# Two chunks of a fused attention and feed-forward kernel on unsplit float32 weights, gates and activations

## Chip, core and metric

The kernel runs on one core of a Trainium2 chip. The metric is the device time of one execution in microseconds. Three executions of the kernel before took 1021.11, 1022.39 and 1024.19 us; the median is 1022.39. A fourth execution was profiled.

## What is computed

Sliding-window attention over 8 batches, 8 heads, 576 positions and 64 dimensions (each position sees itself and the 63 before it), then a feed-forward block with a rational gate on the 4608 tokens. Weights arrive as float64 and q, k, v as float32.

```python
def _attn_ref(q, k, v):
    scores = scale * np.matmul(q, k.transpose(0, 1, 3, 2))
    rel = pos[:, None] - pos[None, :]
    mask = (rel >= 0) & (rel < window)
    scores = np.where(mask, scores, -1000000000.0)
    ...
    attn = attn / (np.sum(attn, axis=-1, keepdims=True) + 1e-09)
    return np.matmul(attn, v)

def _moe_ref(x, w_in, w_out, a, b):
    h = x @ w_in                      # 4608x512 @ 512x2048
    P = a[0] + a[1] * h + a[2] * h2 + a[3] * h3
    Q = 1.0 + np.abs(b[0]) * np.abs(h) + np.abs(b[1]) * h2
    g = P / (Q + 1e-6)
    return g @ w_out                  # 4608x2048 @ 2048x512
```

## The kernel before

**Tiling.** The tokens are cut into 12 chunks of 384. The 2048 columns of the feed-forward block are cut into 16 blocks of 128. A *step* is one block of one chunk: `ffn1` multiplies the chunk's attention output x (four tiles of 128x384) by the block of w_in, the gate follows on ScalarE, VectorE and GpSimd, and three steps later (`LAG`) `ffn2` multiplies the gate's output by the block of w_out and adds it into three PSUM accumulators of 128x512. There are 192 steps. The first two chunks are taken in halves, so that they can begin while the weights still arrive: eight steps of chunk 0, sixteen of chunk 1, eight more of chunk 0, whose first half waits in `part` (L285); from step 32 on a chunk is 16 steps. At a chunk's end ScalarE copies the accumulators to `ob` (L294), and a DMA takes them out.

**Attention** is worked in *units*: two heads of one chunk, four units per chunk. `unit_scores` makes the scores on TensorE (L182), masks them and takes the maximum on VectorE (L188 to L198), six exp on ScalarE (L201), and divides (L203 to L205). `unit_transpose` transposes on TensorE (L212) and copies on ScalarE (L214). `unit_av` multiplies by v (L223). The scores and the transposes share one PSUM buffer, so one unit follows the other. All of these matmuls take plain float32 tiles.

**Precision.** The products of the feed-forward block use float32r tiles, a float32 with a shortened mantissa, in which a value is a pair: hi (the cast) and lo (what the cast left out). A product is three matmuls, lo·hi, hi·hi and hi·lo: L239 twelve times per step, L280 nine times. So each weight, each x and each gate output is cast on ScalarE and subtracted on VectorE: `decode` builds a float32 out of the float64's two words (one pass of ScalarE, L113, four of VectorE, L114 to L118) and splits it at once (L121, L122); `unit_av` does the same for x (L228, L229); the gate makes gh directly (L257) and gl as the rest of the division (L258 to L260).

**Order.** The program is written step by step. `todo` says at which step a weight is loaded or an attention unit begins; the weights of the first half come with steps 0 to 7, those of the second half one load per step from step 7 to step 22. Then a scheduler sets the order in which the instructions stand on each engine; every engine works through its own row in that order. Buffers come from pools: a tile waits until the one whose buffer it takes has been read.

Of the kernel before, what the change touches and what calls it, by code (L numbers as in the profile page):

```python
# [9 lines left out]
F32 = mybir.dt.float32  # L10
# [7 lines left out]
CH = 384  # L18
TC = CH // WIN
PR = TC // 2  # L20
DEC = 28
AHEAD = 3
# [9 lines left out]
def swa_rational_ffn(ctx: ExitStack, tc: tile.TileContext, qT, kT, v, w_in, w_out, a, b, out):  # L32
# [61 lines left out]
    wi_h = const.tile([P, NCC, DFF], F32R, name="wi_h")  # L94
    wi_l = const.tile([P, NCC, DFF], F32R, name="wi_l")
    wo_h = const.tile([P, NF, DO], F32R, name="wo_h")
    wo_l = const.tile([P, NF, DO], F32R, name="wo_l")
# [3 lines left out]
    def decode(src, hi, lo):  # L101

        w = stage.tile([P, 512, 2], U32, name="w_st", bufs=2)
        if len(src.shape) == 3:
            nc.sync.dma_start(out=w.rearrange("p (c n) two -> p c (n two)", c=src.shape[1]), in_=src)
        else:
            nc.sync.dma_start(out=w.rearrange("p n two -> p (n two)"), in_=src)
        low, high = w[:, :, 0], w[:, :, 1]
        c = stage.tile([P, 512], U32, name="w_c")
        cf = c.bitcast(F32)  # L110


        nc.scalar.activation(cf, w.bitcast(F32)[:, :, 1], AF.Abs)  # L113
        nc.vector.tensor_scalar(out=cf, in0=cf, scalar1=2.0 ** -15, scalar2=None, op0=ALU.max)  # L114

        nc.vector.tensor_scalar(out=c, in0=c, scalar1=3, scalar2=0x3FFFFFF8, op0=ALU.logical_shift_left, op1=ALU.bitwise_and)
        nc.vector.scalar_tensor_tensor(out=c, in0=low, scalar=29, in1=c, op0=ALU.logical_shift_right, op1=ALU.bitwise_or)  # L117
        nc.vector.scalar_tensor_tensor(out=c, in0=high, scalar=0xC0000000, in1=c, op0=ALU.bitwise_and, op1=ALU.bitwise_or)  # L118
        if len(hi.shape) == 3:
            cf = cf.rearrange("p (c n) -> p c n", c=hi.shape[1])  # L120
        nc.scalar.copy(out=hi, in_=cf)  # L121
        nc.vector.tensor_tensor(out=lo, in0=cf, in1=hi.bitcast(F32), op=ALU.subtract)  # L122

    def load_w_in(i):
        sl = slice(i * P, (i + 1) * P)
        decode(w_in_v[:, :, 2 * i * P:2 * (i + 1) * P], wi_h[:, :, sl], wi_l[:, :, sl])

    def load_w_out(i):
        decode(w_out_v[:, i, :], wo_h[:, i, :], wo_l[:, i, :])
# [87 lines left out]
    def unit_av(c, hp):  # L217
        u = live.pop((c, hp))

        ps = ps_a.tile([P, TC, WIN], F32, name="ps_x", bufs=1)  # L220
        for j in range(TC):
            for z in range(2):
                nc.tensor.matmul(ps[z * 64:z * 64 + 64, j, :], u["vt"][:, u["vw"][j], z * 64:z * 64 + 64],  # L223
                                 u["pT"][:, z, j * WIN:(j + 1) * WIN], start=True, stop=True)
        xh[c, hp] = xp.tile([P, CH], F32R, name=f"xh{hp}")
        xl[c, hp] = xp.tile([P, CH], F32R, name=f"xl{hp}")
        x = ps.rearrange("p t s -> p (t s)")
        nc.scalar.copy(out=xh[c, hp], in_=x)  # L228
        nc.vector.tensor_tensor(out=xl[c, hp], in0=x, in1=xh[c, hp].bitcast(F32), op=ALU.subtract)  # L229
# [4 lines left out]
    def ffn1(c, i):  # L234
        h = ps_h.tile([P, CH], F32, name="h")
        n = 0
        for cc in range(NCC):
            for w, x in ((wi_h, xl), (wi_h, xh), (wi_l, xh)):
                nc.tensor.matmul(h, w[:, cc, i * P:(i + 1) * P], x[c, cc], start=n == 0, stop=n == 3 * NCC - 1)  # L239
                n += 1  # L240
# [3 lines left out]
        gh = gp.tile([P, CH], F32R, name="gh")  # L244
        gl = gp.tile([P, CH], F32R, name="gl")
# [8 lines left out]

        nc.scalar.activation(ah, u, AF.Ln, bias=QADD)
        nc.scalar.activation(ah, ah, AF.Exp, scale=-1.0)  # L256
        nc.vector.scalar_tensor_tensor(out=gh, in0=num, scalar=a_sb[:, 0:1], in1=ah, op0=ALU.add, op1=ALU.mult)  # L257
# [12 lines left out]
    def ffn2(s):  # L270
# [6 lines left out]
        for t in range(NTS):  # L277
            ts = slice(t * P, (t + 1) * P)
            for n, (g, w) in enumerate(((gl, wo_h), (gh, wo_l), (gh, wo_h))):
                nc.tensor.matmul(acc[c][t], g[:, ts], w[:, i, :], start=first and n == 0, stop=last and n == 2)  # L280
# [3 lines left out]
        if c == 0 and c not in part:  # L284
            part[c] = const.tile([P, NTS, DO], F32, name="part")  # L285
            for t in range(NTS):
                nc.scalar.copy(out=part[c][:, t, :], in_=o[t])
            return
        for t in range(NTS):
            ob = part[0][:, t, :] if s == total - 1 else op.tile([P, DO], F32, name="ob")  # L290
            if c in part:
                nc.vector.tensor_tensor(out=ob, in0=o[t], in1=part[c][:, t, :], op=ALU.add)
# [15 lines left out]
    wi, wo = list(range(H, NF)), list(range(H, NF))  # L308
    queue = [(load_w_in, wi.pop(0)) for _ in range(WLEAD)]
    while wi or wo:  # L310
        if wi:
            queue.append((load_w_in, wi.pop(0)))
        queue.append((load_w_out, wo.pop(0)))
    for n, call in enumerate(queue):
        at(H + n - 1, *call)

# [72 lines left out]
```

## Time and profile before

| | us |
|---|---|
| median of three runs | 1022.39 |
| profiled execution, whole time | 1025.14 |
| its span, first to last instruction | 1023.3 |
| TensorE busy | 953.1 (93%) |
| TensorE weight loads busy | 840.4 (82%) |
| VectorE busy | 850.3 (83%) |
| ScalarE busy | 725.8 (71%) |
| GpSimd busy | 233.7 (23%) |
| mean granted TensorE clock | 0.978 |

Shares of the whole span hide that the run has stages: a stage has to be read by itself, by the engine that is full in it. The busy time of an instruction runs from its start to its end, and neighbours on one engine can overlap; the pace of an engine is read from start to start.

### The profile page before, as it was taken

Reading aid. Unit: us, or ns where it says so; the run is one execution under the profiler, and the core shown is the slowest. Engines: PE = TensorE matmul, PEld = TensorE weight load, DVE = VectorE, ACT = ScalarE, POOL = GpSimd, SP = SyncE. Lnnn points to the kernel's source line nnn. Section 1 sums busy time; section 2 is a strip of 40 time slices with the busy share of each in tenths; the row PEclk is TensorE's granted clock in tenths of the full one; section 3 lists DMA queues with packets and bytes.
Section 4 is the critical chain, followed back from the end, with each engine's and each line's share of the span. In section 5 each row is a group of like instructions: output and inputs, shape, how many; then the busy total and the mean of one; then the engine's idle time right before and its main releaser. Section 6 shows DMA issues by size and latency. Waiting matters only on the chain.

```text
span 1023.3 us, 18244 instructions
## 1 busy us (share of the span) xinstructions
PE 953.1 (93%) x6624; PEld 840.4 (82%) x6624; DVE 850.3 (83%) x1639; ACT 725.8 (71%) x1734; POOL 233.7 (23%) x231
## 2 busy tenths in 40 slices
PE   2677876899999999999999999999999999999997
PEld 2565755788898898898898898898898898888996
DVE  5999999998878878878878878878888888888785
ACT  4675765577767867867867867867867867866664
POOL 2000010002322322322322322322322322322221
PEclk9878989899999999999999999999999999999999
DMA  6634433111112112111112112111112112100000
GB/s 197 205 99 133 133 94 111 50 50 55 60 30 60 61 31 65 64 31 58 60 30 61 61 31 65 64 32 58 60 31 60 62 31 65 65 16 2 31 1 31
DMA packets 68537, 64.09 MB, mean 63 GB/s; under 512 B 4448, under 2 KB 61792, under 8 KB 68448
## 3 DMA queue, kind: packets, MB, share of 16 engines
q1 hardware_dynamic: 68448, 62.93, 19.8%
q8 instruction: 52, 0.85, 0.4%
q14 instruction: 37, 0.30, 0.1%
HBM read 53.48 MB, written 9.44 MB: 61 GB/s over the span
## 4 chain that ended last, share of the span: by engine, by line
PE 81%; DVE 11%; ACT 3%; DMA 3%; issue 1%; POOL 0%; SPq 0%; POOLq 0%; ACTq 0%; DVEq 0%
PE o L280 37%; PE h L239 35%; PE ps_x L223 3%; PE ps_s L182 3%; PE ps_s L212 3%; DMA w_st<-w_in 1%; DVE w_c L117 1%; DMA w_st<-w_out 1%; ACT sm L201 1%; DVE w_c L118 1%; DVE num L259 1%; DVE gh L257 1%; DVE u L258 1%; DVE num L249 1%; DVE num L250 1%
## 5 line engine op out<-in xcount | busy, mean ns | idle before, releaser
L239 PE MATMUL h<-xl,wi_h 128*128 128x384 f32 x768 | 264.9, 345 | 14.8 <-DVE num L250 8.6
L239 PE MATMUL h<-xh,wi_h 128*128 128x384 f32 x768 | 260.6, 339 | 0.0
L239 PE MATMUL h<-xh,wi_l 128*128 128x384 f32 x768 | 259.7, 338 | 0.0
L280 PE MATMUL o<-wo_h,gl 128*128 128x512 f32 x576 | 238.1, 413 | 22.3 <-DVE gl L260 22.3
L252 POOL TENSOR_TENSOR u<-u,ah 128x384 f32<-128x384 f32 x164 | 166.7, 1017 | 317.3 <-ACT u L248 278.7
L280 PE MATMUL o<-wo_h,gh 128*128 128x512 f32 x576 | 231.7, 402 | 0.0
L280 PE MATMUL o<-wo_l,gh 128*128 128x512 f32 x576 | 230.2, 400 | 0.0
L249 DVE TENSOR_TENSOR num<-num,h 128x384 f32<-128x384 f32 x192 | 106.1, 553 | 108.9 <-ACT num L247 108.7
L246 ACT ACTIVATE ah<-h 128x384 f32<-128x384 f32 x192 | 94.3, 491 | 108.1 <-PE h L239 83.3
L205 POOL TENSOR_TENSOR sm<-sm,rs 128x768 f32<-128x768 f32 x40 | 61.7, 1541 | 457.9 <-DVE rs L204 352.3
L201 ACT ACTIVATE sm<-sm,nmx 128x128 f32<-128x128 f32 x288 | 111.9, 390 | 76.4 <-DVE nmx L198 76.4
L239 PEld LDWEIGHTS h<-xl,wi_h 128*128 128x128 f32 x768 | 145.4, 189 | 23.3 <-DVE num L250 11.3
L280 PEld LDWEIGHTS o<-wo_h,gl 128*128 128x128 f32 x576 | 111.3, 193 | 51.3 <-DVE gl L260 24.6
L239 PEld LDWEIGHTS h<-xh,wi_h 128*128 128x128 f32 x768 | 145.5, 189 | 4.6
L239 PEld LDWEIGHTS h<-xh,wi_l 128*128 128x128 f32 x768 | 145.4, 189 | 0.0
L248 ACT ACTIVATE u<-ah,b_sb 128x384 f32<-128x384 f32 x192 | 135.4, 706 | 0.0
L280 PEld LDWEIGHTS o<-wo_h,gh 128*128 128x128 f32 x576 | 111.2, 193 | 26.1
L257 DVE SCALAR_TENSOR_TENSOR gh<-num,a_sb,ah 128x384 fp32r<-128x384 f32 x192 | 114.8, 615 | 17.6 <-ACT ah L256 16.9
L247 ACT ACTIVATE num<-h,a_sb 128x384 f32<-128x384 f32 x192 | 128.2, 668 | 0.0
L280 PEld LDWEIGHTS o<-wo_l,gh 128*128 128x128 f32 x576 | 111.8, 194 | 19.4
L250 DVE SCALAR_TENSOR_TENSOR num<-num,a_sb,h 128x384 f32<-128x384 f32 x192 | 117.9, 614 | 5.9
L259 DVE SCALAR_TENSOR_TENSOR num<-num,a_sb,u 128x384 f32<-128x384 f32 x192 | 115.8, 620 | 0.8
(45 smaller groups left out, 1090.3 us busy)
## 6 DMA issues: line engine op xcount, KB each, us to landing
out<-ob SPq DMA_DIRECT2D x33, 256.0 KB, 2.0
w_st<-w_in SPq DMA_DIRECT2D x16, 512.0 KB, 4.4
w_st<-w_out SPq DMA_DIRECT2D x16, 512.0 KB, 3.6
q<-qT SPq DMA_DIRECT2D x32, 192.0 KB, 3.3
vt<-v SPq DMA_DIRECT2D x16, 384.0 KB, 3.4
vt<-v SPq DMA_DIRECT2D x16, 320.0 KB, 3.9
kt<-kT SPq DMA_DIRECT2D x16, 224.0 KB, 3.6
kt<-kT SPq DMA_DIRECT2D x16, 192.0 KB, 3.6
```

Of the source, the lines that this page charges most:

```text
L201: nc.scalar.activation(sm[:, j, :], sm[:, j, :], AF.Exp, bias=nmx[:, j:j + 1], accum_out=sums[:, j:j + 1])
L205: (nc.vector if c < 2 else nc.gpsimd).tensor_tensor(out=sm, in0=sm, in1=rs.unsqueeze(2).broadcast_to([P, NR, P]), op=ALU.mult)
L239: nc.tensor.matmul(h, w[:, cc, i * P:(i + 1) * P], x[c, cc], start=n == 0, stop=n == 3 * NCC - 1)
L246: nc.scalar.activation(ah, h, AF.Abs)
L247: nc.scalar.activation(num, h, AF.Identity, scale=a_sb[:, 3:4], bias=a_sb[:, 2:3])
L248: nc.scalar.activation(u, ah, AF.Identity, scale=b_sb[:, 1:2], bias=b_sb[:, 0:1])
L249: nc.vector.tensor_tensor(out=num, in0=num, in1=h, op=ALU.mult)
L250: nc.vector.scalar_tensor_tensor(out=num, in0=num, scalar=a_sb[:, 1:2], in1=h, op0=ALU.add, op1=ALU.mult)
L252: (nc.vector if n_gates[0] <= DEC else nc.gpsimd).tensor_tensor(out=u, in0=u, in1=ah, op=ALU.mult)
L257: nc.vector.scalar_tensor_tensor(out=gh, in0=num, scalar=a_sb[:, 0:1], in1=ah, op0=ALU.add, op1=ALU.mult)
L259: nc.vector.scalar_tensor_tensor(out=num, in0=num, scalar=a_sb[:, 0:1], in1=u, op0=ALU.add, op1=ALU.subtract)
L280: nc.tensor.matmul(acc[c][t], g[:, ts], w[:, i, :], start=first and n == 0, stop=last and n == 2)
```

## The change

The first `NX` = 2 chunks, 32 steps, take plain float32 throughout: `ffn1` is four matmuls (L256) in place of twelve, `ffn2` three (L309) in place of nine. For these chunks `unit_av` copies x to a float32 tile without subtracting, and the gate makes one float32 tile g: it refines the reciprocal by one step (L277, L278) and multiplies (L280). `decode` writes a float32 weight and splits nothing. The splitting is a function of its own, `split`, called for one weight per step from step 14 to step 45 (`SPLIT`). Unsplit weights, hi and lo parts and `part` share one ring of 65 buffers; x and g have rings of their own; arriving weights have three buffers (two before), `ob` three (two before).

```diff
+NX = 2
+SPLIT = 14
-    xp = ctx.enter_context(tc.tile_pool(name="xp", bufs=2))
+    xp = ctx.enter_context(tc.tile_pool(name="xp", bufs=16))
-    gp = ctx.enter_context(tc.tile_pool(name="gp", bufs=LAG + 1))
-    op = ctx.enter_context(tc.tile_pool(name="op", bufs=2))
+    gp = ctx.enter_context(tc.tile_pool(name="gp", bufs=2 * (LAG + 1)))
+    op = ctx.enter_context(tc.tile_pool(name="op", bufs=3))
...
+    wp = ctx.enter_context(tc.tile_pool(name="wp", bufs=4 * NF + 1))
...
-    def decode(src, hi, lo):
+    def decode(src, dst):
-        w = stage.tile([P, 512, 2], U32, name="w_st", bufs=2)
+        w = stage.tile([P, 512, 2], U32, name="w_st", bufs=3)
...
-        nc.scalar.copy(out=hi, in_=cf)
-        nc.vector.tensor_tensor(out=lo, in0=cf, in1=hi.bitcast(F32), op=ALU.subtract)
...
+    def split(w, name):
+        hi = wp.tile(list(w.shape), F32R, name=name + "_h", tag="w")
+        lo = wp.tile(list(w.shape), F32R, name=name + "_l", tag="w")
+        nc.scalar.copy(out=hi, in_=w)
+        nc.vector.tensor_tensor(out=lo, in0=w, in1=hi.bitcast(F32), op=ALU.subtract)
+        return hi, lo
...
+        if c < NX:
+            xh[c, hp] = xp.tile([P, CH], F32, name="x", tag="x")
+            nc.scalar.copy(out=xh[c, hp], in_=x)
+            return
...
+            if c < NX:
+                nc.tensor.matmul(h, wi[i][:, cc, :], xh[c, cc], start=cc == 0, stop=cc == NCC - 1)
+                continue
...
+        if c < NX:
+            nc.vector.scalar_tensor_tensor(out=u, in0=u, scalar=QADD, in1=ah, op0=ALU.add, op1=ALU.mult)
+            nc.vector.scalar_tensor_tensor(out=u, in0=u, scalar=2.0, in1=ah, op0=ALU.subtract, op1=ALU.mult, reverse0=True)
+            g = gp.tile([P, CH], F32, name="g", tag="g")
+            nc.vector.scalar_tensor_tensor(out=g, in0=num, scalar=a_sb[:, 0:1], in1=u, op0=ALU.add, op1=ALU.mult)
+            gs[c, i] = g, None
+            return
...
+            if c < NX:
+                nc.tensor.matmul(acc[c][t], gh[:, ts], wo[i], start=first, stop=last)
+                continue
...
+    for i in range(NF):
+        at(SPLIT + 2 * i, split_w_in, i)
+        at(SPLIT + 2 * i + 1, split_w_out, i)
```

The scheduler gives the new program an order of its own. Three places of it follow; a number behind a name tells tiles of one name apart, and x12 stands for twelve such instructions in a row.

On TensorE at the start of chunk 1 (step 8), before: one attention unit (transposes L212, values L223, and the scores L182 of the next) stands between the first nine and the last three products L239 of steps 8 and 9.

```order
L239 MATMUL h<-xh_788,wi_l 128x384
L212 MATMUL ps_s<-ident,sm 128x128 x6
L223 MATMUL ps_x<-pT,vt 64x64 x12
L182 MATMUL ps_s<-kt,q 64x128 x12
L239 MATMUL h<-xl_955,wi_h 128x384
```

The same place now: L256 are the products of steps 8 and 9 and, behind, 10 and 11, L309 those of `ffn2` for chunk 0, L225, L236 and L195 the unit.

```order
L256 MATMUL h<-x,wi 128x384 x2
L309 MATMUL o_802<-wo,g 128x512
L309 MATMUL o_803<-wo,g 128x512
L225 MATMUL ps_s<-ident,sm 128x128 x6
L236 MATMUL ps_x<-pT,vt 64x64 x12
L195 MATMUL ps_s<-kt,q 64x128 x12
L256 MATMUL h<-x,wi 128x384 x10
```

The same three rows of a unit stand once more just ahead of the first row here, between the products for the first two and for the third of the four x tiles: two units lie inside step 8, and before it was one.

On VectorE from the first multiply of the 13th gate (L249) to the end of a split, before: a gate's and a decode's instructions alternate, and the one subtraction L122 follows its own decode.

```order
L249 TENSOR_TENSOR num_1352<-num_1352,h_1337 128x384
L116 TENSOR_SCALAR w_c_1476<-w_c_1476 128x512
L260 TENSOR_TENSOR gl_1302<-num_1300,ah_1298 128x384
L118 SCALAR_TENSOR_TENSOR w_c_1427<-w_st_1425,w_c_1427 128x512
L252 TENSOR_TENSOR u_1351<-u_1351,ah_1350 128x384
L250 SCALAR_TENSOR_TENSOR num_1352<-num_1352,a_sb_90,h_1337 128x384
L117 SCALAR_TENSOR_TENSOR w_c_1476<-w_st_1474,w_c_1476 128x512
L188 SCALAR_TENSOR_TENSOR sm_2115<-ps_s_2102,mask_89 128x384 x2
L249 TENSOR_TENSOR num_1401<-num_1401,h_1386 128x384
L252 TENSOR_TENSOR u_1400<-u_1400,ah_1399 128x384
L118 SCALAR_TENSOR_TENSOR w_c_1476<-w_st_1474,w_c_1476 128x512
L122 TENSOR_TENSOR wo_l_162<-w_c_1427,wo_h_161 128x512
```

Behind the first multiply of the 14th gate now: L135 is the subtraction of a split, L277 to L280 are a gate's end, L246 an x of chunk 2, L201 a unit's mask.

```order
L135 TENSOR_TENSOR wi_l_1859<-wi_735,wi_h_1858 128x512
L277 SCALAR_TENSOR_TENSOR u_1141<-u_1141,ah_1140 128x384
L135 TENSOR_TENSOR wo_l_1912<-wo_924,wo_h_1911 128x512
L246 TENSOR_TENSOR xl_1643<-ps_x_1629,xh_1642 128x384
L135 TENSOR_TENSOR wi_l_1974<-wi_932,wi_h_1973 128x512
L201 SCALAR_TENSOR_TENSOR sm_1692<-ps_s_1679,mask_89 128x384 x2
L135 TENSOR_TENSOR wo_l_2027<-wo_1096,wo_h_2026 128x512
L280 SCALAR_TENSOR_TENSOR g_1122<-num_1111,a_sb_90,u_1110 128x384
L135 TENSOR_TENSOR wi_l_2064<-wi_963,wi_h_2063 128x512
L135 TENSOR_TENSOR wo_l_2101<-wo_1158,wo_h_2100 128x512
L278 SCALAR_TENSOR_TENSOR u_1141<-u_1141,ah_1140 128x384
L135 TENSOR_TENSOR wi_l_2173<-wi_994,wi_h_2172 128x512
```

Seven splits stand among a dozen instructions: the scheduler has drawn splits together and ahead, so that 22 of the 32 stand before the 17th gate.

On ScalarE at the end of a chunk, before: L294 copies the three accumulators, each between instructions of two gates whose products are done (L255 and L256 are Ln and Exp of a gate).

```order
L256 ACTIVATE ah<-ah 128x384
L294 COPY ob<-o_5403 128x512
L255 ACTIVATE ah<-u 128x384
L294 COPY ob<-o_5404 128x512
L256 ACTIVATE ah<-ah 128x384
L214 COPY pT<-ps_s 128x768
L294 COPY ob<-o_5405 128x512
```

The same now, where L327 is the copy, L214 the six exp of an attention unit, L265 to L267 the first instructions of a gate.

```order
L214 ACTIVATE sm,sums<-sm,nmx 128x128 x6
L265 ACTIVATE ah<-h 128x384
L266 ACTIVATE num<-h,a_sb 128x384
L327 COPY ob<-o_4940 128x512
L327 COPY ob<-o_4941 128x512
L327 COPY ob<-o_4942 128x512
L267 ACTIVATE u<-ah,b_sb 128x384
```

The copies stand together, behind the exp of a unit and the beginning of a gate. On TensorE, one step's twelve L260 stand between the last product of a chunk and the first of the next; before, two steps' L239 and a whole unit's matmuls stood there.

More of the change, by code (lines that the diff above doesn't have):

```diff
@@ L237, in ffn1 @@
         for cc in range(NCC):
-            for w, x in ((wi_h, xl), (wi_h, xh), (wi_l, xh)):
-                nc.tensor.matmul(h, w[:, cc, i * P:(i + 1) * P], x[c, cc], start=n == 0, stop=n == 3 * NCC - 1)
+            if c < NX:
+                nc.tensor.matmul(h, wi[i][:, cc, :], xh[c, cc], start=cc == 0, stop=cc == NCC - 1)
+                continue
+            hi, lo = wi[i]
+            for w, x in ((hi, xl), (hi, xh), (lo, xh)):
+                nc.tensor.matmul(h, w[:, cc, :], x[c, cc], start=n == 0, stop=n == 3 * NCC - 1)
                 n += 1
@@ L278, in ffn2 @@
             ts = slice(t * P, (t + 1) * P)
-            for n, (g, w) in enumerate(((gl, wo_h), (gh, wo_l), (gh, wo_h))):
-                nc.tensor.matmul(acc[c][t], g[:, ts], w[:, i, :], start=first and n == 0, stop=last and n == 2)
+            if c < NX:
+                nc.tensor.matmul(acc[c][t], gh[:, ts], wo[i], start=first, stop=last)
+                continue
+            hi, lo = wo[i]
+            for n, (g, w) in enumerate(((gl, hi), (gh, lo), (gh, hi))):
+                nc.tensor.matmul(acc[c][t], g[:, ts], w, start=first and n == 0, stop=last and n == 2)
         if not last:
@@ L284, in ffn2 @@
         if c == 0 and c not in part:
-            part[c] = const.tile([P, NTS, DO], F32, name="part")
+            part[c] = [wp.tile([P, DO], F32, name="part", tag="w") for _ in range(NTS)]
             for t in range(NTS):
-                nc.scalar.copy(out=part[c][:, t, :], in_=o[t])
+                nc.scalar.copy(out=part[c][t], in_=o[t])
             return
         for t in range(NTS):
-            ob = part[0][:, t, :] if s == total - 1 else op.tile([P, DO], F32, name="ob")
+            ob = op.tile([P, DO], F32, name="ob")
             if c in part:
-                nc.vector.tensor_tensor(out=ob, in0=o[t], in1=part[c][:, t, :], op=ALU.add)
+                nc.vector.tensor_tensor(out=ob, in0=o[t], in1=part[c][t], op=ALU.add)
             else:
```

47 lines of the change are left out of this document (24 added, 23 removed).

## Prediction

> **What bounds the kernel now.** I read the slices of the page first, to see which engine is full in which part of the run.
>
> ```profile
> PE   2677876899999999999999999999999999999997
> DVE  5999999998878878878878878878888888888785
> PEclk9878989899999999999999999999999999999999
> ```
>
> One slice is 25.6 us. VectorE is full in slices 2 to 9, and TensorE only from the eighth on. So there are two regimes, and I cut the span at gates: the table of windows, and under it the same stretches for L246 alone, which runs once per step (one ff block of one chunk).
>
> ```profile
> 0.00:49.50 49.50, 24.36 (x276) 19.56 (x280) 37.73 (x74) 26.24 (x77) 6.88 (x27) 0.93 0.66 198
> 49.50:177.50 128.00, 92.87 (x620) 76.80 (x612) 124.03 (x249) 86.48 (x217) 7.22 (x3) 0.89 0.37 115
> 177.50:256.50 79.00, 74.66 (x452) 65.10 (x453) 72.28 (x140) 54.34 (x119) 5.50 (x5) 0.96 0.18 54
> 256.50:333.30 76.80, 76.80 (x554) 68.57 (x553) 63.80 (x124) 56.22 (x138) 21.98 (x20) 1.00 0.17 50
> ...
> 49.50:177.50 128.00, 7.76 (x16) 0.89 0.37 115
> 177.50:256.50 79.00, 7.82 (x16) 0.96 0.18 54
> 256.50:333.30 76.80, 7.87 (x16) 1.00 0.17 50
> ```
>
> The columns are length, then busy time of PE, PE's weight loads, DVE, ACT and POOL. Steps 0 to 15 take 128.0 us: **VectorE** is busy for 124.0 of them, TensorE for 92.9. Steps 16 to 31 take 79.0 us, with TensorE at 74.7 and VectorE at 72.3: both near full. From step 32 on a chunk of 16 steps takes 76.8 us, and **TensorE** never stops. The change touches steps 0 to 31, in which the first two chunks run, plus what the new program order does later.
>
> **What a step costs TensorE.** The timeline of TensorE in the steady part, and three groups:
>
> ```profile
> 488.83 0.39 PE L280 MATMUL o<-wo_h,gl 128*128 128x512 f32 x1
> ...
> 492.72 0.40 PE L280 MATMUL o<-wo_h,gh 128*128 128x512 f32 x1
> 492.95 0.82 PE L212 MATMUL ps_s<-ident,sm 128*128 128x128 f32 x6
> ...
> 495.70 0.34 PE L239 MATMUL h<-xl,wi_h 128*128 128x384 f32 x1
> ...
> 497.61 0.34 PE L239 MATMUL h<-xh,wi_l 128*128 128x384 f32 x1
> 497.87 0.92 PE L223 MATMUL ps_x<-pT,vt 128*64 128x64 f32 x24
> 498.72 0.89 PE L182 MATMUL ps_s<-kt,q 64*64 64x128 f32 x24
> 499.54 0.50 PE L280 MATMUL o<-wo_h,gl 128*128 128x512 f32 x1
> ...
> L212 PE MATMUL ps_s<-ident,sm 128*128 128x128 f32 x288 | 41.4, 282 | 16.2 <-DVE sm L205 5.9 <-DVE sm L192 5.7 <-POOL sm L205 4.1
> ```
>
> The two products that the change replaces: 18 L280 start from 488.83 to 492.72, so one every 3.89/17 = 0.229 us; 12 L239 from 495.70 to 497.61, one every 1.91/11 = 0.174 us. A step holds 12 L239 and 9 L280: 2.09 + 2.06 = **4.15 us**. A chunk is 16 steps and four attention units, so a unit costs (76.8 − 16 × 4.15)/4 = 2.6 us.
>
> The trace shows float32 matmuls only in attention. The code issues 12 at L182 and 12 at L223 per unit and the trace has x24 of each: a float32 matmul leaves **two records**. The six float32 transposes leave x6, one record each; their row lasts 0.82 us with 0.28 us for one, so a pass over 128 columns takes (0.82 − 0.28)/5 = 0.108 us, or 0.84 ns per column. Two such passes give 2 × 384 × 0.84 = 0.65 us for the new L256 and 2 × 512 × 0.84 = 0.87 us for the new L309. **A float32 step then costs 4 × 0.65 + 3 × 0.87 = 5.2 us, 1.05 us more than three reduced products**, although it has a third as many matmuls. No row shows a full-width float32 product, so I keep ends. The low end is one pass (0.33 and 0.44 us, 2.6 us a step), if the two records overlap. The high end is the L182 row: its 12 matmuls of quarter tiles fill the array three times over 128 columns, 384 columns in 499.54 − 498.72 = 0.82 us with start and drain; 4 × 0.82 + 3 × 1.09 = 6.6 us a step. I take 5.2, nearest to a row without waits in it.
>
> The records give a count and a pace, not what the passes are. The Trainium skill, "FP8 and Floating Point Precision", section "TensorE Precision Notes", says that true FP32 needs four passes through the array. At the pace of the reduced products that would be 4 × 0.174 and 4 × 0.229, 5.5 us a step, and 5 us more for steps 16 to 31 than I reckon below; at the pace of the transposes, each of which may itself be two of its passes, it is my figure.
>
> **What VectorE gains.** The rows of what goes and what comes:
>
> ```profile
> L122 DVE TENSOR_TENSOR wo_l<-w_c,wo_h 128x512 fp32r<-128x512 f32 x16 | 10.9, 684 | 0.2
> L229 DVE TENSOR_TENSOR xl<-ps_x,xh 128x384 fp32r<-128x384 f32 x48 | 26.7, 557 | 7.3 <-ACT xh L228 7.3
> L114 DVE TENSOR_SCALAR w_c<-w_c 128x512 f32<-128x512 f32 x32 | 14.9, 466 | 12.8 <-ACT w_c L113 12.8
> L116 DVE TENSOR_SCALAR w_c<-w_c 128x512 uint32<-128x512 uint32 x32 | 13.4, 419 | 0.1
> L118 DVE SCALAR_TENSOR_TENSOR w_c<-w_st,w_c 128x512 uint32<-128x512 uint32 x32 | 21.8, 684 | 0.1
> L257 DVE SCALAR_TENSOR_TENSOR gh<-num,a_sb,ah 128x384 fp32r<-128x384 f32 x192 | 114.8, 615 | 17.6 <-ACT ah L256 16.9
> L258 DVE SCALAR_TENSOR_TENSOR u<-u,gh 128x384 f32<-128x384 f32 x192 | 103.1, 553 | 5.1
> L259 DVE SCALAR_TENSOR_TENSOR num<-num,a_sb,u 128x384 f32<-128x384 f32 x192 | 115.8, 620 | 0.8
> L260 DVE TENSOR_TENSOR gl<-num,ah 128x384 fp32r<-128x384 f32 x192 | 103.0, 553 | 1.6
> ```
>
> The end of a gate was L257 to L260, 2.34 us. It becomes L277 and L278, priced like L258, and L280, priced like L257: 1.72 us, so 0.62 us less. I counted instructions in the order ahead of the 17th gate's first multiply on VectorE. Before: 29 decodes (one lacks its L118, 28 have their L122), 16 gates, 8 L229. Now: 32 decodes, **22 splits**, 16 gates, 2 subtractions for x. Three more decodes, with four more L118: 3 × (0.47 + 0.42 + 0.68) + 4 × 0.68 = +7.4. Six fewer subtractions of weights: −4.1. Sixteen shorter gates: −9.9. Six fewer subtractions of x: −3.3. Net **−9.9 us**, not the −25 us that would stand here with no split ahead of step 16: the splits are written for steps 14 to 45, but the order has 22 of them ahead of step 16. Ahead of the 33rd gate the same count gives −3 × 0.68 − 32 × 0.62 − 8 × 0.56 = −26 us.
>
> **Steps 0 to 15.** They are VectorE's, so up to 9.9 us go, if it is kept fed. Against that stands the first piece of the order shown above: two whole attention units stand on TensorE between the first half of step 8 and its end, where there was one. What a unit's chain (scores, maximum, exp, division, transposes, values) takes from one to the next shows in its transposes:
>
> ```profile
> 35.43 1.48 PE L212 MATMUL ps_s<-ident,sm 128*128 128x128 f32 x6 [2.23 <-DVE sm L192]
> ...
> 42.23 0.89 PE L212 MATMUL ps_s<-ident,sm 128*128 128x128 f32 x6
> ...
> 71.50 0.82 PE L212 MATMUL ps_s<-ident,sm 128*128 128x128 f32 x6
> ...
> 89.24 0.85 PE L212 MATMUL ps_s<-ident,sm 128*128 128x128 f32 x6
> ```
>
> That is 6.8 us with nothing beside it, and 17.7 us between gates and decodes. The scores have one PSUM buffer, so units do not overlap. VectorE has two gates and a few decodes for such a time; then it waits. The term runs from −9.9 (the unit is covered) to −9.9 + 17.7 = +7.8; I take the middle of the two chains, 12.3 us, which makes **+2.4 us**.
>
> **Steps 16 to 31.** Here TensorE was nearly full, and now each step costs it more: 16 × 5.2 + 2 units × 2.6 (the order has two there, as before) = 88.4 us for 79.0: **+9.4 us**. VectorE, relieved by another 16 us here, would have been ready sooner and is no help. With 6.6 us a step it is +32; with 2.6 TensorE needs 47 us and VectorE, at 72.3 − 16 = 56, sets the pace: about −20.
>
> **From step 32 on** the instructions are those of before but for three splits, 2 us of VectorE beside 13 us of its idle time per chunk. The order has moved, though, where one chunk's accumulators are copied out, and the next chunk's first L313 must wait for the first copy. The timeline of ScalarE there:
>
> ```profile
> 484.74 0.40 ACT L201 ACTIVATE sm<-sm,nmx 128x128 f32<-128x128 f32 x1 [2.05 <-DVE nmx L198]
> ...
> 486.98 0.18 ACT L201 ACTIVATION_READ_ACCUMULATOR sm<-sm,nmx 128x1 f32 x1
> 487.26 0.49 ACT L246 ACTIVATE ah<-h 128x384 f32<-128x384 f32 x1
> 487.65 0.67 ACT L247 ACTIVATE num<-h,a_sb 128x384 f32<-128x384 f32 x1
> ...
> 491.78 0.59 ACT L294 COPY ob<-o 128x512 f32<-128x512 f32 x1
> ```
>
> Before, the six exp ran 8 us ahead of the chunk's last L280 (492.72), and 6.8 us of other matmuls lay between it and the next chunk's first (499.54). Now six exp and two gate instructions stand directly ahead of the copies, and on TensorE one step's twelve products (2.1 us) are the only cover. Exp 2.4 (484.74 to 487.16), L246 and L247 0.39 + 0.67, the copy 0.59: if they begin only when the chunk ends, TensorE waits 4.1 − 2.1 = 2.0 us; if ScalarE is early, nothing. There are nine such ends after step 32. Behind that L313 on TensorE stand the rest of the products and the next step's, so its wait delays all. I take a third, 0.7 us each, **+6 us**, since before ScalarE stood ready 0.9 us early (491.78 against 492.72). The range is 0 to +18.
>
> Costed at nothing: the casts (L121, 32 × 0.61 us, now L134) and the third buffer for arriving weights, since ScalarE has 41 us to spare in the 128 us of steps 0 to 15; without that cover, what is behind a cast is a gate, and up to 0.6 us per split would show. The rings for x, g and the weights: from the sixteenth split on, a split takes the buffer of 65 allocations earlier, an unsplit weight that is already split and read; without that cover it would hold the gates behind it on ScalarE and VectorE for up to a step, 5 us.
>
> **The sum.** +2.4 + 9.4 + 6 = **+17.8 us** on the profiled execution, whose time is 1025.1 us (span 1023.3): 1042.9. The three runs' median is 1022.4, 2.7 us less; on that scale **1040 us**.
>
> **Rivals.**
> - *Faster: the two records of a float32 matmul overlap.* For it: VectorE's relief of 26 us up to step 32 is real, and step 0 to 31 take 207 us where TensorE is busy 168. Against it: the paced rows. TensorE no longer binds when a step costs under (79.0 − 5.2)/16 = 4.6 us. Then −26 + 12 (the unit) + 6 = −8 us: 1014.
> - *No change.* The added unit is covered, the copies are early: −9.9 + 9 + 0, 1022. For it: ScalarE has idle time everywhere. Against it: both are in the order.
> - *Dearer products.* The pace of the L182 row holds at full width: 2 + 32 + 6 = +40, 1062. Against it: that row has start and drain in it.
>
> Chances: forecast 0.70, faster 0.13, no change 0.09, dearer 0.08. A measurement of this kernel tells about 0.3% from no change, 3 us: faster 0.13, same 0.09, slower 0.78. The range leaves out the faster rival and most of the dearer one: 1019 to 1060.
>
> **What would show it.** In the changed profile: two records per L256 and L309, starting about 0.33 and 0.43 us apart; steps 16 to 31 in 88 us, TensorE never idle; idle time of VectorE around the first gates of step 8; L135 spread over steps 8 to 31; a wait of L313 for ob once per chunk. If steps 16 to 31 take less than 79 us, the price of float32 is wrong; if steps 0 to 15 take under 120, the unit was covered; if the chunks from step 48 on still take 76.8, the copies were.

## Result and profile after

The changed kernel takes **1053.01 us** (median of four runs, 1051.56 to 1053.56), the kernel before beside it on the same chip 1022.13: a ratio of **1.029** (95% interval 1.027 to 1.031). It is slower, as forecast, and by more: 31 us for a forecast of 18. The profiled executions (1051.6 and 1025.1 us, spans 1049.7 and 1023.3) lie 26.4 us apart, and it is this difference that can be laid out by stages. Of the 13 us by which 1053.0 lies above the forecast of 1040, the stages below account for 8.6 (26.4 for 17.8); the rest is the choice of executions, since the profiled one lay 2.7 us above its median before and 1.5 below it after.

The busy tenths of the page after the change:

```profile
PE   3589677999999999999999999999999999999997
DVE  5799899667788788788788788788788788888886
PEclk9899899999999999999999999999999999999999
```

TensorE is full from the eighth slice on, and VectorE falls to 6, 6 and 7 in slices 8 to 10, where it was at 9, 9 and 8 before. So the relief of VectorE is real, and there TensorE has no room for it. The windows of the changed kernel, cut ahead of the gates of steps 0, 6, 8 and 16 (columns as in the prediction: length, then busy time of PE, weight loads, DVE, ACT, POOL):

```profile
53.50:91.50 38.00, 32.06 (x177) 17.43 (x176) 36.39 (x76) 28.85 (x75) 0.00 (x0) 0.96 0.53 168
91.50:119.40 27.90, 24.11 (x154) 13.12 (x152) 21.62 (x44) 14.61 (x38) 0.00 (x0) 0.94 0.37 117
119.40:181.00 61.60, 45.05 (x204) 23.70 (x205) 59.67 (x117) 46.17 (x111) 4.41 (x3) 0.92 0.29 94
```

The same stretches of the kernel before:

```profile
49.50:98.70 49.20, 34.38 (x266) 28.93 (x258) 47.63 (x98) 33.27 (x87) 0.00 (x0) 0.86 0.41 130
98.70:114.50 15.80, 12.32 (x93) 10.52 (x94) 15.77 (x32) 11.21 (x29) 0.00 (x0) 0.88 0.36 104
114.50:177.50 63.00, 46.17 (x263) 37.35 (x261) 60.63 (x121) 41.99 (x101) 7.22 (x3) 0.92 0.34 107
```

Steps 0 to 5 are 11.2 us shorter. Steps 6 and 7 are 12.1 us longer: VectorE works 5.9 us more in them and is idle for 6.3 us. Steps 8 to 15 are again VectorE's (59.67 of 61.60). From step 16 on, after the change (cut ahead of steps 16, 32, 48, 64 and 80):

```profile
181.00:269.50 88.50, 88.50 (x334) 46.50 (x333) 60.38 (x114) 54.19 (x119) 6.90 (x6) 1.00 0.08 26
269.50:350.00 80.50, 79.36 (x554) 68.00 (x554) 69.81 (x126) 56.97 (x139) 23.64 (x20) 1.00 0.16 48
350.00:428.00 78.00, 77.35 (x554) 68.45 (x553) 64.91 (x122) 56.74 (x140) 23.71 (x20) 1.00 0.17 52
428.00:506.00 78.00, 77.35 (x554) 68.46 (x553) 64.81 (x121) 56.77 (x140) 23.73 (x20) 1.00 0.16 50
```

| stretch | before | after | difference | forecast |
|---|---|---|---|---|
| up to the first gate | 49.5 | 53.5 | +4.0 | 0 |
| steps 0 to 15 | 128.0 | 127.5 | −0.5 | +2.4 |
| steps 16 to 31 | 79.0 | 88.5 | +9.5 | +9.4 |
| step 32 to the end | 766.8 | 780.2 | +13.4 | +6 |
| sum | 1023.3 | 1049.7 | +26.4 | +17.8 |

The new products show their price directly. The timeline of TensorE in steps 16 to 31 (start, length, instruction):

```profile
229.27 4.45 PE L309 MATMUL o<-wo,g 128*128 128x512 f32 x10
233.66 0.44 PE L195 MATMUL ps_s<-kt,q 64*64 64x128 f32 x6
234.03 5.43 PE L256 MATMUL h<-x,wi 128*128 128x384 f32 x16
239.29 1.02 PE L309 MATMUL o<-wo,g 128*128 128x512 f32 x2
```

Each matmul leaves two records: 16 of L256 lie in 239.29 − 234.03 = 5.26 us, 0.33 each, and 10 of L309 in 4.39 us, 0.44 each with the switch to another kind of matmul behind them. Where no switch lies between, the records' starts are 0.3225 and 0.4295 us apart: 0.645 and 0.859 us per matmul, 5.16 us a step.

At the end of a chunk, the timeline of ScalarE:

```profile
595.79 0.47 ACT L265 ACTIVATE ah<-h 128x384 f32<-128x384 f32 x1
596.16 0.66 ACT L266 ACTIVATE num<-h,a_sb 128x384 f32<-128x384 f32 x1
596.72 1.53 ACT L327 COPY ob<-o 128x512 f32<-128x512 f32 x3
```

And of TensorE there (in brackets its idle time, and what ended it):

```profile
596.35 0.34 PE L260 MATMUL h<-xh,wi_l 128*128 128x384 f32 x1
597.34 0.50 PE L313 MATMUL o<-wo_h,gl 128*128 128x512 f32 x1 [0.65 <-ACT ob L327]
597.68 0.39 PE L313 MATMUL o<-wo_l,gh 128*128 128x512 f32 x1
```

The copies stand behind exp and two gate instructions, and L313 waits 0.65 us for the first of them. From start to start the wait costs more: 1.33 us lie between the first row and the third, and without a wait it would be 0.17 + 0.23 = 0.40, so **0.93 us**.

### The profile page after: what moved, and what is told of

The parts are those of the page before. It is cut to its first block, busy times and chain, and to the rows that moved or that the text cites. A ratio compares the mean times of both kernels' runs of the same rounds, so it can differ in the third digit from the quotient of the medians.

```text
span 1049.7 us, 17833 instructions
## 1 busy us (share of the span) xinstructions
PE 981.3 (93%) x6400; PEld 793.8 (76%) x6400; DVE 861.0 (82%) x1599; ACT 719.7 (69%) x1734; POOL 248.1 (24%) x231
## 4 chain that ended last, share of the span: by engine, by line
PE 81%; DVE 10%; DMA 4%; ACT 3%; issue 1%; SPq 0%; POOL 0%; DVEq 0%; ACTq 0%
PE o L313 31%; PE h L260 31%; PE o L309 5%; PE h L256 5%; PE ps_x L236 3%; PE ps_s L195 3%; DMA w_st<-w_in 3%; PE ps_s L225 2%; DMA w_st<-w_out 1%; DVE wi_l L135 1%; DVE wo L119 1%; DVE nmx L211 1%; DVE wo_l L135 1%; DVE wo L120 1%; DVE num L269 1%
## 5 line engine op out<-in xcount | busy, mean ns | idle before, releaser
L260 PE MATMUL h<-xl,wi_h 128*128 128x384 f32 x640 | 217.8, 340 | 0.0
L260 PE MATMUL h<-xh,wi_l 128*128 128x384 f32 x640 | 216.0, 337 | 0.0
L260 PE MATMUL h<-xh,wi_h 128*128 128x384 f32 x640 | 215.0, 336 | 0.0
L313 PE MATMUL o<-wo_h,gl 128*128 128x512 f32 x480 | 191.8, 400 | 9.9 <-ACT ob L327 5.3
L313 PE MATMUL o<-wo_h,gh 128*128 128x512 f32 x480 | 189.8, 395 | 0.0
L313 PE MATMUL o<-wo_l,gh 128*128 128x512 f32 x480 | 189.8, 395 | 0.0
L268 DVE TENSOR_TENSOR num<-num,h 128x384 f32<-128x384 f32 x192 | 105.5, 549 | 75.9 <-ACT num L266 75.9
L273 ACT ACTIVATE ah<-u 128x384 f32<-128x384 f32 x192 | 100.2, 522 | 83.1 <-POOL u L271 70.8
L265 ACT ACTIVATE ah<-h 128x384 f32<-128x384 f32 x192 | 93.1, 485 | 85.2 <-DVE gl L289 34.9
L214 ACT ACTIVATE sm<-sm,nmx 128x128 f32<-128x128 f32 x288 | 111.8, 390 | 57.5 <-DVE nmx L211 57.5
L267 ACT ACTIVATE u<-ah,b_sb 128x384 f32<-128x384 f32 x192 | 135.3, 705 | 0.0
L286 DVE SCALAR_TENSOR_TENSOR gh<-num,a_sb,ah 128x384 fp32r<-128x384 f32 x160 | 104.3, 652 | 27.3 <-ACT ah L274 26.9
L260 PEld LDWEIGHTS h<-xl,wi_h 128*128 128x128 f32 x640 | 120.2, 188 | 6.6 <-DVE num L269 0.4
L260 PEld LDWEIGHTS h<-xh,wi_h 128*128 128x128 f32 x640 | 120.2, 188 | 6.0 <-issue 0.2
L260 PEld LDWEIGHTS h<-xh,wi_l 128*128 128x128 f32 x640 | 120.1, 188 | 0.3
L269 DVE SCALAR_TENSOR_TENSOR num<-num,a_sb,h 128x384 f32<-128x384 f32 x192 | 117.2, 611 | 3.8
L313 PEld LDWEIGHTS o<-wo_h,gl 128*128 128x128 f32 x480 | 90.2, 188 | 32.9 <-ACT ob L327 7.9
L256 PE MATMUL h<-x,wi 128*128 128x384 f32 x256 | 96.9, 526 | 16.0 <-DVE num L269 12.1
L289 DVE TENSOR_TENSOR gl<-num,ah 128x384 fp32r<-128x384 f32 x160 | 101.4, 634 | 7.8 <-PE ps_s L225 0.5
```

The lines of the kernel that those rows point to most:

```text
L214: nc.scalar.activation(sm[:, j, :], sm[:, j, :], AF.Exp, bias=nmx[:, j:j + 1], accum_out=sums[:, j:j + 1])
L256: nc.tensor.matmul(h, wi[i][:, cc, :], xh[c, cc], start=cc == 0, stop=cc == NCC - 1)
L260: nc.tensor.matmul(h, w[:, cc, :], x[c, cc], start=n == 0, stop=n == 3 * NCC - 1)
L267: nc.scalar.activation(u, ah, AF.Identity, scale=b_sb[:, 1:2], bias=b_sb[:, 0:1])
L268: nc.vector.tensor_tensor(out=num, in0=num, in1=h, op=ALU.mult)
L269: nc.vector.scalar_tensor_tensor(out=num, in0=num, scalar=a_sb[:, 1:2], in1=h, op0=ALU.add, op1=ALU.mult)
```

## Experiments

Each starts from the changed kernel if nothing else is said. e1 to e4 shared the runs of the kernel before, so did e5 to e8, and e9 to e11; it took 1023.9 to 1024.2 us there, and 1022.1 beside the changed kernel. So a difference of 2 us between times of different groups says nothing; where it matters, compare the ratios to the kernel before.

**e1: the price of float32 taken away.** The operands of the first two chunks are bfloat16, each product is issued three times.

```diff
-            xh[c, hp] = xp.tile([P, CH], F32, name="x", tag="x")
+            xh[c, hp] = xp.tile([P, CH], BF16, name="x", tag="x")
...
+                for r in range(3):
+                    nc.tensor.matmul(h, wi[i].bitcast(BF16)...[:, cc, :, 1], xh[c, cc], ...)
```

> The changed kernel with the products of the first two chunks on bfloat16 operands, each issued three times, so that the output of these chunks is not the reference's. A step then costs TensorE 12 x 0.174 + 9 x 0.229 = 4.15 us, as before the change, and everything else of the change stays: unsplit weights, one subtraction less per gate, the late splits. If the price of float32 makes steps 16 to 31 long, they fall from 88.5 us to 73 to 79 (TensorE 16 x 4.15 + 2 x 2.6 = 72, VectorE 60), and the time to 1035 to 1042, or lower by another 8 to 10 if the new order also has the copies of the accumulators early. Rival: the order and VectorE beside GpSimd make that stage long: it stays at 86 to 89 us, the time at 1050 to 1054.

Measured: 1024.9 us, ratio 1.001 (1.000 to 1.002). Its window of steps 16 to 31:

```profile
176.50:250.00 73.50, 72.86 (x446) 39.51 (x453) 58.57 (x109) 51.92 (x116) 5.88 (x5) 1.00 0.10 32
```

73.5 us in place of 88.5, with TensorE still full: the rival falls, and the price of float32 is TensorE's. The time is that of the lower case, at its end: beside the 15 us here, the gates' times show 3.4 us gained at the start, 3.7 in steps 32 to 47 and 2.9 in steps 48 to 175, since the order changed in these places too. Steps 0 to 15 changed by under 1 us: float32's price doesn't show there.

**e2 and e8: another order at the chunks' ends, and its control.**

```diff
-AHEAD = 3
+AHEAD = 2
```

> The changed kernel with AHEAD = 2 in place of 3: each attention unit begins one step later, the work is the same, and in the order no exp of a unit stands directly ahead of the copies of the accumulators on ScalarE. If the place of the copies costs what chunks have lost from step 32 on, a chunk from step 80 on takes 76.8 to 77.0 us (78.0 now), steps 0 to 31 take what they take now, and the time is 1042 to 1046. Rival: VectorE's instructions that stretch beside GpSimd cost it: they stay, a chunk stays at 78, the time at 1051 to 1054.

> The kernel before with AHEAD = 2, the control for e2. If e2 gained because of where the copies of the changed order stand, the same edit gives nothing here: a chunk takes 76.8 us, the time is 1022 to 1027. Rival: starting units a step later is worth 7 us in itself: 1015 to 1018.

Measured: e2 1045.8 us, 7.2 less than the changed kernel; e8, the same edit on the kernel before, 1024.9 (ratio 1.0005, 0.999 to 1.002), no change. So it is not the edit as such that helps, but what it undoes in the new order. Two chunks of e2 from step 112 on, and under it what TensorE waited for in them (us in total, times, longest):

```profile
656.60:811.50 154.90, 154.22 (x1106) 136.81 (x1105) 132.15 (x240) 112.79 (x279) 47.03 (x40) 1.00 0.17 50
```

```profile
PE o L313 <- DVE gl L289: 0.7, 2, 0.5
```

77.45 us a chunk, not 76.8: the wait for ob is gone, and a smaller one for gl stands in its place. The time lies in the expected range, but not for the expected reason alone: of the 6.7 us between the profiled executions, 6.0 were gained in steps 32 to 79 and only 1.2 from step 80 on, where seven chunks of 76.8 to 77.0 us would have gained 7 or more (the first 32 steps were 0.6 longer).

**e3: the copies on VectorE.**

```diff
-                nc.scalar.copy(out=ob, in_=o[t])
+                nc.vector.tensor_copy(out=ob, in_=o[t])
```

> The changed kernel with the copies of the accumulators to ob on VectorE in place of ScalarE; the order up to step 48 stays as it is. If the copies are late because they stand behind exp and gate instructions on ScalarE, the waits of L313 for ob (9 x 0.59 us) go, a chunk from step 64 on takes 76.8 to 77.2 us in place of 78.0, and the time is 1042 to 1046. Rival: the switches between kinds of matmul, or VectorE itself, cost the 1.2 us: a chunk stays at 78, or gets longer by the 3 x 0.6 us of new work on VectorE, and the time is 1051 to 1056.

Measured: 1071.9 us, 19 more than the changed kernel, a miss beyond both cases. What TensorE waited for in two chunks (592.5 to 753.7 us):

```profile
PE o L313 <- DVE gl L289: 3.0, 2, 1.5
PE o L313 <- DVE ob L327: 1.9, 2, 0.9
```

The wait for ob moved with the copies to VectorE, and the gate's gl, behind them in the same row, became late too. A chunk takes 80.6 us. VectorE, 65 us busy of 78, was not free at the moment at which it was needed.

**e4: two buffers for arriving weights.**

```diff
-        w = stage.tile([P, 512, 2], U32, name="w_st", bufs=3)
+        w = stage.tile([P, 512, 2], U32, name="w_st", bufs=2)
```

> The changed kernel with two buffers for arriving weights, as before the change, in place of three. If the third buffer makes the start late (weights are fetched ahead of q, k and v), the first gate comes at about 50 us in place of 54, and the time falls by about 4 us, to 1048 to 1050, if the later stages stay as they are. Rival: the start is late for another reason: the first gate stays at 53 to 54 us, and the time moves only by what two buffers do to the decodes in steps 0 to 15.

Measured: 1051.2 us; the first gate stays at 53.6 us, as the rival said. But steps 8 to 15 and 16 to 23 changed places:

```profile
119.50:169.60 50.10, 41.30 (x199) 22.38 (x198) 48.44 (x96) 36.28 (x83) 3.32 (x2) 0.93 0.44 141
169.60:222.70 53.10, 47.62 (x183) 24.77 (x182) 48.37 (x89) 36.86 (x86) 2.94 (x2) 1.00 0.08 26
```

The order now has 8 splits and 30 decodes ahead of the 17th gate where it had 22 and 32. Steps 8 to 15 lost 11.5 us, VectorE's busy time in them 11.2: there VectorE's work is time. Steps 16 to 23, 44.5 us in the changed kernel, got 8.6 longer, with 15 splits in a bunch.

**e6: the splits held back.** The cast takes a zero that the gate of its step has made, so that the order can't draw it ahead.

```diff
-        nc.scalar.copy(out=hi, in_=w)
+        nc.scalar.activation(hi, w, AF.Identity, bias=zero[0])
...
+        if HOLD <= n_gates[0] <= 48:
+            zero[0] = zp.tile([P, 1], F32, name="zero")
+            nc.vector.tensor_scalar(out=zero[0], in0=ah[:, 0:1], scalar1=0.0, scalar2=None, op0=ALU.mult)
```

> The changed kernel with each split held back to its step: the cast of a split takes a zero that the gate of its step makes, and the splits are written for steps 16 to 47. In the order 26 decodes and no split stand ahead of the 17th gate (32 and 22 in the changed kernel), 16 splits ahead of the 33rd. If VectorE sets the pace of steps 8 to 15 and the splits drawn ahead gave its relief back, 22 x 0.68 + 6 x 2.25 = 28 us of its work leave these steps, and they end 11 to 18 us sooner, until TensorE binds; steps 16 to 31 stay TensorE's with 88 to 95 us, and the time is 1037 to 1045. Rival: the attention units, not VectorE, set the pace of these steps: step 16 comes at 177 to 181 us as it does now, and the time is at 1050 or above.

Measured: 1044.9 us, 8.2 less. Its windows of steps 8 to 15 and 16 to 31:

```profile
122.20:165.30 43.10, 38.96 (x161) 21.02 (x162) 35.53 (x69) 28.99 (x70) 2.94 (x2) 0.92 0.27 85
165.30:261.20 95.90, 95.90 (x390) 50.66 (x389) 81.63 (x166) 66.57 (x146) 8.26 (x7) 1.00 0.16 49
```

Steps 8 to 15 are 18.5 us shorter and now nearer to TensorE's 39.0 us than to VectorE's 35.5. So the relief had been given back to splits and decodes drawn ahead. 7.4 us of it are lost again in steps 16 to 31, where TensorE is full and now has 56 more matmul records (390 for 334), 40 of them attention's.

**e5: the gates off GpSimd**, on e2.

```diff
-DEC = 28
+DEC = 200
```

> The kernel of e2 with every gate's multiply u by ah on VectorE (DEC = 200 in place of 28), so that GpSimd has only the four divisions of a chunk. VectorE gets 16 x 0.55 = 8.9 us of work per chunk in exchange. In e2 a chunk still took 77.4 us, against 76.8 before the change, and the first L313 of a step waited up to 0.7 us for gl, while L286 and L289 averaged 695 and 653 ns instead of 615 and 553. If they are long because GpSimd's multiply runs beside them, they return to 615 and 553 here, the wait for gl goes, a chunk takes 76.8 us, and the time is 4 to 6 us under e2 (1040 to 1042). Rival: VectorE's own order makes gl late: with 9 us more on VectorE a chunk takes 78 us or more, the time 1048 or more.

Measured: 1040.4 us, 5.4 less than e2. Two chunks from step 112 on, and under it the group of the gate's last instruction in them:

```profile
655.40:809.10 153.70, 153.70 (x1106) 137.05 (x1105) 148.00 (x273) 112.62 (x278) 11.78 (x9) 1.00 0.16 51
```

```profile
L289 DVE TENSOR_TENSOR gl<-num,ah 128x384 fp32r<-128x384 f32 x33 | 28.3, 856 | 1.9
```

TensorE never stops, and a chunk takes 76.85 us, as before the change, although VectorE has 8 us more work in it. The wait for gl is gone and L286 is back at 613 ns. But L289, which was to return to 553 ns, got longer, 856 ns on average, beside GpSimd's divisions, and holds nobody up: a long L289 alone isn't the wait. Whether the multiplies beside it or the order that changed with them made gl late in e2 isn't separated by this run.

**e11: e6, e2 and e5 together.**

> The changed kernel with e6 (splits held), e2 (AHEAD = 2) and e5 (gates on VectorE) together. If the three are separate terms, they add: 1053.0 - 8.2 - 7.2 - 5.4 = 1032, within 3, and chunks from step 80 on take 76.8 us; what is left above the time before is the price of float32 in 32 steps, 32 x 1.0, less VectorE's relief. Rival: the gains overlap, or VectorE, with the gates' multiplies and the held splits together, becomes the bound in steps 28 to 47: 1037 or more.

Measured: 1033.9 us, ratio 1.009 (1.007 to 1.011): they add, within 2 us, and a chunk from step 80 on takes 76.8 us. By the ratios they add too: 1.0286 less 0.0075, 0.0080 and 0.0041 leaves 1.0090, and 1.0091 was measured. What is left above the kernel before is not what was expected, float32's price less VectorE's relief. Cut at the gates, the profiled executions differ by +3.2 us at the start, −18.4 in steps 0 to 15, +15.3 in steps 16 to 31, +9.4 in steps 32 to 63 and −2.3 after that. So the first 32 steps together are 3.1 us shorter than before, and the loss stands at the start and in steps 32 to 63, where 15 of the held splits now lie and TensorE waits 5.4 us for VectorE.

**e7, e9, e10: float32 where VectorE binds.** Chunk 0 alone in float32, chunks straight, and GpSimd multiplies from the fifth gate on.

```diff
-DEC = 28
+DEC = 4
-NX = 2
+NX = 1
-AHEAD = 3
+AHEAD = 4
-    phases = [(0, 0, H), (1, 0, H), (1, H, NF), (0, H, NF)] + [(c, 0, NF) for c in range(2, NCH)]
+    phases = [(c, 0, NF) for c in range(NCH)]
...
-        at(SPLIT + 2 * i, split_w_in, i)
-        at(SPLIT + 2 * i + 1, split_w_out, i)
+        at(15 + i, split_w_in, i)
+        at(18 + i, split_w_out, i)
```

> Float32 for chunk 0 alone and the chunks taken straight, 16 steps each, so that no chunk waits half done; splits at the step that needs them, units one step earlier (AHEAD = 4), GpSimd multiplies from the fifth gate on. If the change's relief of VectorE is worth its price only where VectorE binds, steps 0 to 15 take 98 to 108 us from the first gate (128 before the change), steps 16 to 31, with reduced products and all 32 splits beside them, 80 to 92 (79 before), and a chunk 76.8 to 77.5: 1000 to 1012 in all, faster than before the change. Rival: the splits, now all in steps 16 to 31, and GpSimd beside VectorE cost more than float32 saves: 1020 to 1030.

> e7 with the output of chunk 0 copied and written like that of every other chunk (e7 put it aside in part and never wrote it): three copies of 0.6 us on ScalarE and three DMAs more, in steps 16 to 19. The copies are ScalarE's, which has time to spare there: the time is 1015 to 1019, a ratio of 0.991 to 0.996, and the stages are e7's within 2 us. Rival: the copies stand behind exp and gate instructions like those of e3 and hold L309 or L313: steps 16 to 23 get longer by 3 us or more, and the time is 1020 to 1024, no better than before the change.

> The kernel before with the other edits of e9 and no float32: chunks taken straight, AHEAD = 4, GpSimd multiplies from the fifth gate on. If float32 products for chunk 0, with the splits put off, make e9 faster, this one is no better than before the change: 1020 to 1027. Rival: the straight order and GpSimd's earlier work make it: 1012 to 1017, as e9 or below.

Measured: e7, which doesn't write chunk 0, took 1015.9 us. That is a miss, above its 1000 to 1012, although its two stages (101.9 and 90.2 us from gate to gate) and its chunk (76.9) lie in their ranges: the first gate came 5.1 us later than before the change, and the upper ends of the stages sum to about 1024 even with the old start. e9, which writes chunk 0, took **1017.2 us**, ratio **0.993** (0.991 to 0.994) to the kernel before: faster than both kernels, by little but clear of the scatter. Its time is the expected one; its stages are 2.5 us longer and 3.4 shorter than e7's, not within 2. e10, which has the straight order, earlier units and earlier GpSimd multiplies without float32, and like e7 leaves chunk 0 unwritten, took 1026.7 (1.002, 1.001 to 1.003): the other edits alone gain nothing. The windows of e9, steps 0 to 15 and 16 to 31:

```profile
55.50:160.00 104.50, 92.28 (x435) 50.57 (x434) 102.84 (x203) 78.85 (x187) 18.41 (x13) 0.95 0.42 129
160.00:246.70 86.70, 78.87 (x536) 65.14 (x535) 77.96 (x140) 63.06 (x152) 24.32 (x20) 0.98 0.15 45
```

Steps 0 to 15 take 104.5 us in place of 128.0, the splits and the reduced products then 86.7 in place of 79.0, and the start is 6.0 us later.

**e12: a third buffer for v.**

```diff
-        vt = kv.tile([P, TC, P], F32, name="vt")
+        vt = kv.tile([P, TC, P], F32, name="vt", bufs=3)
```

> The changed kernel with three buffers for v in place of two. At 42.4 us SyncE's queue held the DMA of v for the next unit until L236 had read a buffer, and the DMA of w_out behind it; ScalarE's L115 for that weight waited 4.4 us at the head of its row, and the copy pT, on which TensorE waited 4.1 us, stood behind L115. If that chain makes the start late, the DMA of v waits for nothing now, the copy pT is not held, and step 0's gate comes at 50 to 51.5 us in place of 54; the time falls by up to 4 us where the later stages keep their lengths. Rival: the transfers themselves are late: the gate stays at 53 to 56 us.

Measured: 1060.3 us, the first gate at 54.3 us. The edit shortened the wait but didn't take it away: the scheduler used the buffer to fetch v one unit earlier, and the next fetch waited 2.1 us in SyncE's queue where it had waited 4.4, with w_out behind it. That weight was issued 0.8 us sooner (at 42.55 us) and landed only 0.1 sooner (47.71). ScalarE in e12:

```profile
47.73 0.66 ACT L115 ACTIVATE wo<-w_st 128x512 f32<-128x512 f32 x1 [4.34 <-DMA w_st<-w_out]
48.29 0.79 ACT L227 COPY pT<-ps_s 128x768 f32<-128x768 f32 x1
```

Steps 8 to 15, reordered, became 5.9 us longer. The theory of the start was not settled by this: the rival, a transfer that is late in itself, stays possible.

## Why the prediction was right, and where it was too small

**The price of float32: right.** Two records per matmul, 5.16 us a step for a forecast of 5.2, +9.5 us in steps 16 to 31 for +9.4; e1 takes the price away and the stage gives back 15. The records follow each other at full length, so the rival in which they overlap falls, and so does the dearer one. The Trainium skill's rule of four passes ("FP8 and Floating Point Precision", section "TensorE Precision Notes") fits this trace, in which passes can't be counted: 0.645 us over 4 x 384 columns and 0.859 over 4 x 512 would both be 0.42 ns per column and pass, a little under the 0.45 of the reduced products (0.174 over 384), so that the 5.5 us that I set beside the sum was too high by their difference in pace.

**VectorE's relief and the added unit: right in kind, near in sum by luck.** Forecast −9.9 and +12.3, together +2.4; measured −0.5. The −11.2 us of steps 0 to 5 and the +12.1 of steps 6 and 7 look like these two terms and are not. VectorE's work fell by 11.2 us in the first stretch but rose by 5.9 in the second; over steps 0 to 15 it fell from 124.0 to 117.7 us, by 6.4 (by 8.3 with what stands ahead of the first gate). VectorE's idle time rose from 4.0 to 9.8 us, by 5.9 where the unit was to cost 12.3. Both terms were too large, and the errors cancelled. VectorE's long waits in steps 6 and 7:

```profile
103.52 1.02 DVE L205 SCALAR_TENSOR_TENSOR sm<-ps_s,mask 128x384 f32<-128x384 f32 x2 [1.31 <-PE ps_s L195]
...
108.02 0.17 DVE L216 TENSOR_SCALAR sums<-sums 128x6 f32<-128x6 f32 x1 [2.49 <-ACT sm L214]
...
111.30 0.43 DVE L116 TENSOR_SCALAR wi<-wi 128x512 f32<-128x512 f32 x1 [1.90 <-ACT wi L115]
```

The first two, 3.8 us, are the unit's chain, scores and exp, as the step said. The third isn't: this L115 stands on ScalarE behind the copies of chunk 0's sums to `part`. And the stretch ends with one more such wait. On ScalarE an L115 waits 4.25 us for its weight, until 118.84, and the gate of step 8 behind it begins at 119.91, although TensorE was done with the products there at 118.0. That relief is given back in steps 8 to 15 by splits and decodes drawn ahead is shown by e4 and e6.

**From step 32 on: mis-sized.** The term was +6 and measured +13.4. The wait for the copies is there at eight chunk ends, 0.65 to 0.74 us each; I had taken 0.7 at nine, a third of the worst case, and that it came so close is luck. What the term left out: a steady chunk lost 1.2 us. From start to start the wait costs 0.93 of it. The rest lies mostly in switches: TensorE's next start comes about 0.1 us later behind a return from attention's matmuls and 0.09 later at a switch from a product to L236 or L195, and two chunks have 18 such returns where they had 16. Between L260 and L313 a switch adds nothing. And steps 32 to 47 lost 3.7 us. `ffn2` runs three steps late, so three steps of float32 L309 fall behind step 32: 9 x (0.859 − 0.687) = 1.5 us. A wait for gl in chunk 2's second `ffn2` cost 1.3 more:

```profile
285.44 0.40 PE L313 MATMUL o<-wo_h,gh 128*128 128x512 f32 x1
286.96 0.49 PE L313 MATMUL o<-wo_h,gl 128*128 128x512 f32 x1 [1.13 <-DVE gl L289]
```

I had taken the chunk's end for a single wait, and everything else of the new order for free. e5 and e11 show that a steady chunk goes back to 76.8 us in another order, with the gates' multiply on VectorE; e2, with the later units alone, got to 77.45.

**The start: missed, and read only from the trace.** +4.0 us came where I forecast nothing: the sum has no term ahead of the first gate, and ScalarE's spare time, by which I costed the third weight buffer at nothing, doesn't say what stands behind a weight that is late. The third buffer alone isn't the cause, since with two the start was as late (e4). ScalarE ahead of the first gate, before the change:

```profile
43.45 0.68 ACT L113 ACTIVATE w_c<-w_st 128x512 f32<-128x512 f32 x1 [0.61 <-DMA w_st<-w_out]
44.03 0.78 ACT L214 COPY pT<-ps_s 128x768 f32<-128x768 f32 x1
```

And after it:

```profile
42.75 0.69 ACT L115 ACTIVATE wi<-w_st 128x512 f32<-128x512 f32 x1
47.85 0.66 ACT L115 ACTIVATE wo<-w_st 128x512 f32<-128x512 f32 x1 [4.42 <-DMA w_st<-w_out]
48.42 0.78 ACT L227 COPY pT<-ps_s 128x768 f32<-128x768 f32 x1
```

And TensorE behind it:

```profile
49.25 1.41 PE L236 MATMUL ps_x<-pT,vt 128*64 128x64 f32 x24 [4.14 <-ACT pT L227]
```

A weight's L115 waits for its transfer at the head of ScalarE's row, and the copy pT, for which TensorE waits 4.1 us, stands behind it. In e1, where pT waits for TensorE alone, the gate came at 50.6 us. The traces of the other runs sort in the same way: wherever behind 40 us an L115 waits over 4 us with an attention copy behind it (in e4 the copy of x behind a wait of 5.4 us), the first gate comes at 52.7 to 56.3 us, and in e1, e8 and e10, which have no such row there, at 50.6 to 51.2. No run took the chain away by itself, so that it is the cause is argued and not shown, and what would bring the start back stays open.

## What to carry to other kernels

A float32 product with a third of the matmuls can cost TensorE more than three reduced ones, so it pays only in a stage that another engine sets: here two chunks of it lost 29 in 1000 as first ordered and 9 in 1000 in the best order tried, and the first chunk alone, with the chunks straight, won 7 in 1000. Work taken off a full engine is gone only if the scheduler can't refill the place with work drawn ahead; count what stands ahead of the next stage. A scheduler that gets a changed program may reorder the untouched part as well: compare a steady chunk's time before and after, here 76.8 and 78.0 us.

## What was unexpected

VectorE stretched beside GpSimd. The timeline of GpSimd in e5:

```profile
711.55 1.47 POOL L218 TENSOR_TENSOR sm<-sm,rs 128x768 f32<-128x768 f32 x1 [17.74 <-DVE rs L217]
```

And of VectorE:

```profile
708.95 0.56 DVE L289 TENSOR_TENSOR gl<-num,ah 128x384 fp32r<-128x384 f32 x1
...
711.30 0.55 DVE L268 TENSOR_TENSOR num<-num,h 128x384 f32<-128x384 f32 x1
711.76 1.68 DVE L289 TENSOR_TENSOR gl<-num,ah 128x384 fp32r<-128x384 f32 x1
```

L268, which reads h in PSUM, runs beside the division in its usual 0.55 us, but it had started first. L289, with both inputs in SBUF, starts 0.2 us behind the division and ends at 713.44, 0.42 us after the division's end (713.02), as if it had stood still until GpSimd was done. Eight of the 32 L289 in these two chunks do so, at 1.67 to 1.68 us; the other 24, with no GpSimd beside them, take 0.56. The changed kernel has the comparison that is missing here: between 506 and 971 us, L268 and L269, which both read PSUM, started 39 and 70 times while GpSimd was in an instruction and kept their 0.55 and 0.61 us, while the 14 L289 that did so took 0.84 to 1.36 and each ended 0.41 to 0.42 us after the GpSimd instruction. That is what the Trainium skill says in "SBUF — State Buffer", section "SBUF: two separate sides": the port pair that the two engines share is an exclusive lock for a whole instruction, which a VectorE operation with two SBUF inputs needs too; these rows agree.
